# First two units of retention in chunks of 128 tokens, the first weight tiles by halves, the first tile's products begun on half of X, and accumulators evacuated in pairs

## The chip, the cores and the metric

One core of one Trainium2 chip runs the kernel. Its engines are TensorE (PE in the profile; its weight loads are PEld), VectorE (DVE), ScalarE (ACT), GpSimd (POOL) and the queue of DMA issues (SP). The metric is the device time of one execution in microseconds (us); less is better.

## The reference, cut to what matters

```
ret = (q @ k.T / 8) * gamma[h] ** (i - j), zero where j > i     # 4 batches, 8 heads, 576 tokens, head size 64
x   = (ret @ v), heads side by side                             # 2304 x 512
x   = leaky_relu(x @ w_in, 0.01) @ w_out                        # 512 -> 2048 -> 512
out = silu(x @ w2_in) @ w2_out                                  # 512 -> 2048 -> 512
```

The matrices of the two layers arrive as 64-bit floats; everything else is float32.

## The kernel before, in words

**Units.** Retention is done in chunks of 64 tokens (`CH`). A unit is one batch's first 256 tokens (A) or last 320 (B). For each unit and each group `g` of four heads (two pairs `p`) PE makes scores and the chunks' k-v products (`products`; tile `r`), DVE multiplies the scores with a mask of decays (`pt`) and chains the states chunk by chunk (`decay`; `first`, `st`, `sa`), PE makes the outputs (`outer`, `values`; tile `o`), and DVE scales them into `X`. k is scaled beforehand (`scale_k`, on ACT for the very first group, on POOL for the other three). The first two units, A of batch 0 (`u0`) and A of batch 1 (`u1`), fill the first 512 columns of `X`; each has two groups, so there are four group steps before the matrix products of the layers can have all of `X`. The remaining units are worked in between products later on, at places given by the list `ATT_AT`; a unit's loads stand at times in `free`.

**Layers.** A step `t` handles one of 16 slices `f` of the 2048 hidden values for one block of up to 512 tokens. Every float32 operand is split into a high part (`fp32r`, a CAST on ACT) and a remainder (a subtraction on DVE or POOL), and a product is three passes: high by high, high by remainder, remainder by high. `gemm1` makes `h` (four row pieces `c` of `X`, split as `xs`, three passes each: 12 products), `activate` makes `g`, and `gemm2` adds to four accumulators `acc` (12 products) with a lag of `LAG` = 2 steps, so PE's order is h0, h1, h2, acc of 0, h3, acc of 1, h4, and so on. Accumulators live by twos in two PSUM tiles; after the last slice each is copied out, even ones by ACT and odd ones by DVE.

**Weights.** A slice's 64-bit weights (`w`, 128x1024 numbers, 1 MB) come as two DMAs and are decoded to float32 (`wraw`): a scaling on ACT, clamping and shifting on DVE (half of it by an ACT relu), and one combining instruction on DVE (L340). The first half of `wraw` is w_in (split as `wi`), the second w_out (`wo`). For the first 32 steps the order on every engine is the order of the code (`manual_schedule`); behind that a scheduler decides. In the first 16 steps each step also decodes one slice for two steps later. Three buffers hold 64-bit weights, so that a load waits for the decoding three slices back.

`busy` products compute nothing that is used.

Of the kernel before, what the change touches and what calls it, by code (L numbers as in the profile page):

```python
# [23 lines left out]

BUSY = 3
NP = H // 2
# [7 lines left out]
NC = 2 * H + NP  # L34
# [30 lines left out]
def retention_mlp_kernel(ctx: ExitStack, tc: tile.TileContext, qkva, qkvb, w1, w2, consts, out):  # L65
# [26 lines left out]
    gs_sb = cst[:, 2 * H:NC]  # L92
# [68 lines left out]
    def scale_k(u, p):  # L161
        k = raw[u, p][3]
        if (u, p // 2) == (UNITS[0], 0) or u == UNITS[2]:
            for j in range(2):
                nc.scalar.mul(out=k[:, :, j], in_=k[:, :, j], mul=gk_sb[:, 2 * p + j:2 * p + j + 1])
        else:
            engine = nc.gpsimd if u in UNITS[:2] else nc.vector
            g = gk_sb[:, 2 * p:2 * p + 2].unsqueeze(1).unsqueeze(3)
            engine.tensor_tensor(out=k, in0=k, in1=g.to_broadcast(list(k.shape)), op=ALU.mult)

    def products(u, ps):
# [29 lines left out]
        first = u in UNITS[:2]  # L201
        if first:

            st = st_p.tile([128, 2, 64], F32, tag="first", name="first", bufs=4)
            nc.vector.tensor_copy(out=st, in_=t[:, 0, o:o + 256].rearrange("p (i n) -> p i n", i=2)[:, :, :64])
# [15 lines left out]
        if first:
            last[u, ps] = t[:, 1, o:o + 256].rearrange("p (i n) -> p i n", i=2)[:, :, 64:]

    def leave(u, ps):

        x = st_p.tile([128, 2, 64], F32, tag="last", name="last", bufs=4)
        nc.scalar.copy(out=x, in_=last.pop((u, ps)))
        ends.extend((prep[u, p][1], x[:, i], p) for i, p in enumerate(ps))
# [5 lines left out]
    def outer(u, g):  # L234
# [10 lines left out]
        engine = nc.vector if u in UNITS[:2] else nc.gpsimd  # L245
        y = engine.memset(st_p.tile([128, 1], F32, tag="done", name="done"), 0.0)
# [48 lines left out]
    def load_w(layer, f):  # L295

        if layer == 1 and f < 2:
            w = ld_p.tile([128, 1024], F32, tag="ld", name="wraw")
        else:
            w = wraw_p.tile([128, 1024], F32, tag="wraw", name="wraw")  # L300
        wraw[layer, f] = w
        r = dec_p.tile([128, 1024, 2], I32, tag="w64", name="w64")
        src = (w1, w2)[layer][f].bitcast(I32)
        halves = [slice(0, 512), slice(512, 1024)]
        loads = []
        for c in halves:
            loads.append(nc.sync.dma_start(out=r[:, c].rearrange("p n t -> p (n t)"), in_=src[:, 2 * c.start:2 * c.stop]))
        for c in halves if (layer, f) == (0, 0) else [slice(0, 1024)]:
            wdec.append((w[:, c], r[:, c]))
        return loads[0]  # L310
# [32 lines left out]
    def split_wi(layer, i, f):  # L343
# [3 lines left out]
        return split(w[:, 0], w[:, 1], wraw[layer, f][:, :512], nc.gpsimd if (layer, i, f) == (0, 0, 0) else nc.vector)  # L347
# [309 lines left out]
```

## Time and profile before

| | us |
|---|---|
| median of 3 runs (lowest, highest) | 880.05 (879.78, 881.25) |
| the profiled execution | 880.94 |
| its span, first to last instruction | 879.2 |
| PE busy in it | 855.6 |
| mean granted TensorE clock | 0.998 |

The profiled execution is 1.7 us longer than its span, and 0.9 us longer than the median of the runs. Times below count from the start of the span.

### The profile page before, as it was taken

The numbers are of one execution on the slowest core, as the hardware profiler recorded it, in microseconds if no ns is written. First come the engines' busy times: TensorE is split into PE (matmuls) and PEld (weight loads), VectorE is DVE, ScalarE is ACT, GpSimd is POOL, SyncE is SP. The second block draws the span as 40 slices with busy tenths as digits, with TensorE's granted clock in tenths as the row PEclk, the third lists the DMA queues.
The fourth block names the chain that finished last, engine by engine and source line by source line (L and its number), as shares of the span: only waits on it lengthen the run. The fifth ranks groups of instructions, "written<-read, shape, count | busy, mean of one in ns | idle before, by whom it ended". The sixth has DMA issues, their size and how long they took to land.

```text
span 879.2 us, 14579 instructions
## 1 busy us (share of the span) xinstructions
PE 855.6 (97%) x6000; PEld 717.5 (82%) x6000; DVE 535.3 (61%) x928; ACT 442.8 (50%) x766; POOL 10.5 (1%) x27
## 2 busy tenths in 40 slices
PE   4899999999999999999999999999999999999997
PEld 4578778998877877888999888888888888888896
DVE  4688875576455564446999554654465445544575
ACT  2687754454333443445666444544454445444564
POOL 2100000000000000000000000000000000000000
PEclk9999999999999999999999999999999999999999
DMA  7576541221012010101561000010001000100010
GB/s 294 205 258 229 186 160 57 87 83 57 1 59 87 24 52 30 48 1 48 193 238 49 1 0 1 1 48 1 1 1 48 1 0 1 48 1 0 25 25 25
DMA packets 17826, 58.75 MB, mean 67 GB/s; under 512 B 2016, under 2 KB 2144, under 8 KB 17760
## 3 DMA queue, kind: packets, MB, share of 16 engines
q1 hardware_dynamic: 17760, 57.82, 18.8%
q8 instruction: 47, 0.77, 0.4%
q14 instruction: 19, 0.16, 0.1%
HBM read 53.09 MB, written 4.72 MB: 66 GB/s over the span
## 4 chain that ended last, share of the span: by engine, by line
PE 91%; DVE 1%; ACT 1%; issue 0%; DVEq 0%
PE acc L129 44%; PE h L129 43%; PE o L129 2%; PE r L129 2%; DVE wraw L340 0%; ACT X L414 0%; DVE st L231 0%; DVE g L108 0%; DVE y L418 0%; ACT g L107 0%; ACT wo L107 0%; DVE wi L108 0%; ACT hs L384 0%; ACT y L420 0%; DVE xs L108 0%
## 5 line engine op out<-in xcount | busy, mean ns | idle before, releaser
L129 PE MATMUL h<-xs,wi 128*128 128x512 f32 (+3 forms) x1920 | 432.6, 370 | 1.9 <-ACT wi L107 1.8
L129 PEld LDWEIGHTS h<-xs,wi 128*128 128x128 f32 x1920 | 341.9, 188 | 61.5 <-ACT wi L107 2.7
L129 PE MATMUL acc<-g,wo 128*128 128x512 f32 (+2 forms) x960 | 218.4, 372 | 1.4 <-ACT X L414 1.4
L129 PE MATMUL acc<-wo,g 128*128 128x512 f32 x864 | 212.8, 390 | 0.7 <-ACT y L420 0.7
L129 PEld LDWEIGHTS acc<-g,wo 128*128 128x128 f32 x960 | 171.5, 188 | 28.7 <-ACT X L414 2.2
L129 PEld LDWEIGHTS acc<-wo,g 128*128 128x128 f32 x864 | 161.0, 188 | 33.8 <-ACT y L420 1.1
L107 ACT CAST wo<-wraw 128x512 fp32r<-128x512 f32 x160 | 99.4, 621 | 136.4 <-PE acc L129 136.2
L108 DVE TENSOR_TENSOR wo<-wraw,wo 128x512 fp32r<-128x512 f32 x160 | 110.4, 690 | 94.2 <-ACT wo L107 93.5
L108 DVE TENSOR_TENSOR wi<-wraw,wi 128x512 fp32r<-128x512 f32 x159 | 109.2, 687 | 54.0 <-ACT wi L107 51.9
L387 DVE TENSOR_TENSOR hs<-h,hs 128x512 f32<-128x512 f32 (+1 forms) x80 | 51.0, 638 | 107.2 <-ACT hs L386 107.1
L108 DVE TENSOR_TENSOR g<-hs,g 128x512 fp32r<-128x512 f32 (+3 forms) x160 | 101.6, 635 | 17.0 <-ACT g L107 12.9
L386 ACT ACTIVATE hs<-h 128x512 f32<-128x512 f32 (+1 forms) x80 | 44.4, 555 | 122.2 <-PE h L129 122.0
L107 ACT CAST wi<-wraw 128x512 fp32r<-128x512 f32 x160 | 98.1, 613 | 15.2 <-DVE wraw L340 15.2
L107 ACT CAST g<-hs 128x512 fp32r<-128x512 f32 (+3 forms) x160 | 93.5, 584 | 11.2 <-DVE hs L387 10.6
L384 ACT ACTIVATE hs<-h 128x512 f32<-128x512 f32 (+2 forms) x80 | 44.3, 554 | 107.1 <-PE h L129 104.6
L319 ACT ACTIVATE wraw<-w 128x1024 f32<-128x1024 f32 (+1 forms) x33 | 36.7, 1111 | 14.5 <-DVE wo L108 8.3
L324 DVE TENSOR_SCALAR w<-w 128x512 uint16<-128x512 uint32 (+1 forms) x32 | 33.5, 1047 | 12.1 <-ACT wraw L319 12.0
L340 DVE SCALAR_TENSOR_TENSOR wraw<-w,wraw 128x1024 int32<-128x1024 int32 (+1 forms) x33 | 39.3, 1190 | 1.6 <-ACT w L330 1.4
L107 ACT CAST xs<-X 128x512 fp32r<-128x512 f32 (+3 forms) x40 | 22.7, 578 | 6.5 <-DVE X L275 5.1
L108 DVE TENSOR_TENSOR xs<-X,xs 128x512 fp32r<-128x512 f32 (+3 forms) x38 | 23.5, 635 | 3.3 <-ACT xs L107 3.1
L330 ACT ACTIVATE w<-w,seven 128x512 uint16<-128x512 uint32 (+1 forms) x15 | 23.0, 1535 | 0.0
L129 PEld LDWEIGHTS r<-qkv 64*64 64x64 f32 x896 | 15.5, 134 | 8.2 <-issue 4.6
(55 smaller groups left out, 241.4 us busy)
## 6 DMA issues: line engine op xcount, KB each, us to landing
w<-in_w SPq DMA_DIRECT2D x64, 512.0 KB, 4.6
qkv<-in_qkvb SPq DMA_DIRECT2D x16, 672.0 KB, 5.4
qkvk<-in_qkva SPq DMA_DIRECT2D x16, 256.0 KB, 5.2
qkv<-in_qkva SPq DMA_DIRECT2D x8, 512.0 KB, 4.3
out<-y SPq DMA_DIRECT2D x15, 256.0 KB, 2.0
out<-y SPq DMA_DIRECT2D x6, 128.0 KB, 2.4
cst<-in_consts SPq DMA_DIRECT2D x1, 138.0 KB, 2.2
```

Source lines behind the costliest of these rows:

```text
L107: yield nc.scalar.copy(out=hi, in_=src)
L108: yield engine.tensor_tensor(out=lo, in0=src, in1=hi.bitcast(F32), op=ALU.subtract)
L129: return nc.tensor.matmul(out, lhsT, rhs, start=start, stop=stop)
L319: yield nc.scalar.mul(out=w, in_=hi.bitcast(F32), mul=2.0 ** -112)
L324: yield nc.vector.tensor_scalar(out=end[:, c], in0=lo[:, c].bitcast(U32), scalar1=2.0 ** -29, scalar2=7.0, op0=ALU.mult, op1=ALU.min)
L330: yield nc.scalar.activation(out=end[:, c], in_=lo[:, c].bitcast(U32), func=AF.Relu, scale=-2.0 ** -29, bias=seven)
L340: yield nc.vector.scalar_tensor_tensor(out=wi, in0=hi, scalar=-0x7FFFFFF9, in1=wi, op0=ALU.bitwise_and, op1=ALU.bitwise_xor)
L384: yield nc.scalar.activation(out=hs[:, :n], in_=h[:, :n], func=AF.Prelu, alpha=0.01)
L386: yield nc.scalar.activation(out=hs[:, :n], in_=h[:, :n], func=AF.Sigmoid)
L387: yield nc.vector.tensor_tensor(out=hs[:, :n], in0=h[:, :n], in1=hs[:, :n], op=ALU.mult)
```

## The change

For the first two units, chunks are 128 tokens long. Scores become products of 128x128 (`scores2`), masked with a new 128-wide mask (`mask2`, made by POOL and DVE at the start); the only state inside a unit is the first chunk's k-v product, copied by ACT (`states2`, tile `kv`), and the outputs are 64x128 products (`values2`) scaled with `gq2`, which POOL makes. The state at a unit's end is worked out later (`end2`). The `busy` products between them go; four of them, on a zeroed tile, stand at PE's start. Weight slice 0 is decoded by halves as before; slices 1 and 2 are loaded and decoded by halves, the first halves (w_in) ahead. The first six products of h0 stand behind the last output group in PE's order, and X's other half is split meanwhile. The split of `wi` for slice 0 moves behind the scaling of k on POOL, and that of slice 1 goes to POOL too. `evacuate` copies accumulators out in pairs, and blocks of two accumulators use one from each PSUM tile. k of a later unit is scaled right behind the work ahead of it (`at + 0.05`).

```diff
-NC = 2 * H + NP
+NC = 4 * H + 3 * NP
...
+    mask2 = wraw_p.tile([128, H, 128], F32, tag="wraw", name="mask2")
+    nc.vector.memset(mask2, 1.0)
+    nc.gpsimd.affine_select(
+        out=mask2, in_=mask2, pattern=[[0, H], [1, 128]], compare_op=ALU.is_ge, fill=0.0, base=0, channel_multiplier=-1)
+    gq2 = g_p.tile([128, NP, 2, CH], F32, tag="g", name="gq2")
...
+        gk = gk2_sb if u in UNITS[:2] else gk_sb
...
+    def scores2(u, g):
+
+        s = banks(u, "r")
+        ps = 2 * g, 2 * g + 1
+        for i, p in enumerate(ps):
+            q, k, _, _ = raw[u, p]
+            for c in range(2):
+                cs = slice(c * 128, (c + 1) * 128)
+                for j in range(2):
+                    mm(s[:, j, i * 256 + c * 128:i * 256 + (c + 1) * 128], k[HALF[j], cs], q[HALF[j], cs], True, True)
+        pt = ld_p.tile([128, 2, 2, 2, 128], F32, tag="ld", name="pt")
+        for i, p in enumerate(ps):
+            y = nc.vector.tensor_tensor(
+                out=pt[:, i], in0=s[:, :, i * 256:(i + 1) * 256].rearrange("p j (c n) -> p j c n", n=128),
+                in1=mask2[:, 2 * p:2 * p + 2].unsqueeze(2).to_broadcast([128, 2, 2, 128]), op=ALU.mult)
+        prep[u, g, "pt"] = pt
+        return y
+
+    def states2(u, g):
+        kv = ps_p.tile([128, 512], F32, tag="ps", name="kv")
+        for i in range(2):
+            _, _, v, kn = raw[u, 2 * g + i]
+            for c in range(2):
+                for j in range(2):
+                    mm(kv[HALF[j], (2 * i + c) * 64:(2 * i + c + 1) * 64], kn[:, c, j], v[:, c, j], True, True)
+        x = st_p.tile([128, 2, 2, 64], F32, tag="first", name="first", bufs=4)
+        nc.scalar.copy(out=x, in_=kv[:, :256].rearrange("p (i c n) -> p i c n", c=2, n=64))
+        prep[u, g, "kv"] = x
+        for i in range(2):
+            ends.append((u[1], 2 * g + i, x[:, i]))
+
+    def values2(u, g):
+        o = banks(u, "o")
+        pt, x = prep[u, g, "pt"], prep[u, g, "kv"]
+        for c in range(2):
+            for j in range(2):
+                for i in range(2):
+                    mm(o[HALF[i], j, c * 128:(c + 1) * 128], raw[u, 2 * g + i][2][:, c, j], pt[:, i, j, c], c == 0, False)
+        for i in range(2):
+            for j in range(2):
+                mm(o[HALF[i], j, 128:256], x[HALF[j], i, 0], raw[u, 2 * g + i][0][HALF[j], 128:256], False, True)
+        y = X[:, 2 * g:2 * g + 2, POS[u]:POS[u] + CA]
+        nc.vector.tensor_tensor(
+            out=y.rearrange("p j (c n) -> p j c n", n=128), in0=o[:, :, :CA].rearrange("p j (c n) -> p j c n", n=128),
+            in1=gq2[:, 2 * g:2 * g + 2].rearrange("p a c n -> p a (c n)").unsqueeze(2).to_broadcast([128, 2, 2, 128]),
+            op=ALU.mult)
...
+        nc.vector.scalar_tensor_tensor(
+            out=sa, in0=x[:, 0], scalar=gs2_sb[:, p:p + 1], in1=x[:, 1], op0=ALU.mult, op1=ALU.add)
...
+    def load_w(layer, f, parts=(0, 1), x=None):
...
+        for i in parts:
+            y = nc.sync.dma_start(out=w64[layer, f][:, i * 512:(i + 1) * 512].rearrange("p n t -> p (n t)"),
+                                  in_=src[:, i * 1024:(i + 1) * 1024])
+            if x is not None:
+                behind(y, x)
+        if len(parts) == 2:
+            wdec.append((wraw[layer, f], w64[layer, f]))
+
+    def half(f, i, by_act):
+
+        c = slice(i * 512, (i + 1) * 512)
+        return decode(wraw[0, f][:, c], w64[0, f][:, c], by_act)
...
-        return split(w[:, 0], w[:, 1], wraw[layer, f][:, :512], nc.gpsimd if (layer, i, f) == (0, 0, 0) else nc.vector)
+        return split(w[:, 0], w[:, 1], wraw[layer, f][:, :512], nc.gpsimd if (layer, i) == (0, 0) and f < 2 else nc.vector)
...
-            t = [acc_p.tile([128, 2, 512], F32, tag=f"acc{m}", name=f"acc{m}") for m in range((nt + 1) // 2)]
-            acc[layer, i] = [t[m // 2][:, m % 2] for m in range(nt)]
+            t = [acc_p.tile([128, 2, 512], F32, tag=f"acc{m}", name=f"acc{m}") for m in range(2)]
+
+            acc[layer, i] = [t[m // 2][:, m % 2] if nt > 2 else t[m][:, 0] for m in range(nt)]
...
-            if f < NF - 1:
-                yield
-                continue
-            if layer == 0:
-                if m % 2:
-                    nc.vector.tensor_copy(out=X[:, m, p0:p0 + n], in_=a[:, :n])
-                else:
-                    nc.scalar.copy(out=X[:, m, p0:p0 + n], in_=a[:, :n])
-            else:
-                y = y_p.tile([128, 512], F32, tag="y", name="y")
-                if m % 2:
-                    nc.vector.tensor_copy(out=y, in_=a)
-                else:
-                    nc.scalar.copy(out=y, in_=a)
-                for o, ln, r in rows_of(p0 + m * 128, 128):
-                    nc.sync.dma_start(out=out[r:r + ln], in_=y[o:o + ln])
+            if f == NF - 1 and (m % 2 or nt < 3):
+                for e in (m,) if nt < 3 else (m - 1, m):
+                    evacuate(layer, p0, n, e, acc[layer, i][e])
             yield
...
+    def evacuate(layer, p0, n, m, a):
+        if layer == 0:
+            y = X[:, m, p0:p0 + n]
+            a = a[:, :n]
+        else:
+            y = y_p.tile([128, 512], F32, tag="y", name="y")
+        if m % 2:
+            nc.vector.tensor_copy(out=y, in_=a)
+        else:
+            nc.scalar.copy(out=y, in_=a)
+        if layer == 1:
+            for o, ln, r in rows_of(p0 + m * 128, 128):
+                nc.sync.dma_start(out=out[r:r + ln], in_=y[o:o + ln])
...
+    nw = 3
...
-    nc.vector.memset(warm[:, :1], 0.0)
+    nc.vector.memset(warm, 0.0)
     nc.scalar.copy(out=warm[:, :1], in_=warm[:, :1])
...
+    def busy(n, size=256):
+
+        for _ in range(n):
+            mm(t[:, :size], warm[:, :128], warm[:, :size], True, True)
+
     u0, u1 = UNITS[:2]
     nc.sync.dma_start(out=cst, in_=consts)
-    more_weights(1)
+    load_w(0, 0, (0,))
+    load_w(0, 0, (1,))
     for g in range(NG):
         for u in (u0, u1):
             for p in (2 * g, 2 * g + 1):
                 load(u, p)
+    load_w(0, 1, (0,))
+    busy(3, 512)
+    busy(1)
     nc.vector.tensor_tensor(
-        out=mask, in0=mask, in1=gn_sb.unsqueeze(2).to_broadcast([128, H, CH]), op=ALU.mult)
-    decodes()
-    more_weights(2)
+        out=mask2, in0=mask2, in1=gn2_sb.unsqueeze(2).to_broadcast([128, H, 128]), op=ALU.mult)
+    nc.gpsimd.tensor_copy(out=gq2[:, :, 0], in_=gq_sb)
+    nc.gpsimd.tensor_tensor(
+        out=gq2[:, :, 1], in0=gq_sb, in1=gr_sb.unsqueeze(2).to_broadcast([128, NP, CH]), op=ALU.mult)
+    for i in range(2):
+        run(half(0, i, 0))
...
     scales(u0, 0)
-    run(split_wi(0, 0, 0))
     scales(u1, 0)
     scales(u0, 1)
     scales(u1, 1)
-    sums(u0, 0)
-    leave(u0, (0, 1))
-    outer(u0, 0)
-    values(u0, 0)
-    sums(u1, 0)
-    leave(u1, (0, 1))
-    outer(u1, 0)
-    sums(u0, 1)
-    leave(u0, (2, 3))
-    x = values(u1, 0)
-
-    more_weights(4, x)
+    scores2(u0, 0)
+    states2(u0, 0)
+    run(split_wi(0, 0, 0))
+    values2(u0, 0)
+    scores2(u1, 0)
+    states2(u1, 0)
+    scores2(u0, 1)
+    values2(u1, 0)
+    states2(u0, 1)
+    values2(u0, 1)
     for c in range(2):
         split_x(0, 0, c)
-    outer(u0, 1)
-    busy(1)
-    sums(u1, 1)
-    second = decode(*wdec.pop(0), 1024)
+    x = scores2(u1, 1)
+
+    for n, (f, i) in enumerate(((2, 0), (1, 1), (2, 1))):
+        load_w(0, f, (i,), x if n == 0 else None)
+    states2(u1, 1)
+    second = half(1, 0, 512)
     next(second)
     next(second)
-    busy(2)
-    values(u0, 1)
-    outer(u1, 1)
-    next(second)
-    busy(2)
-    values(u1, 1)
-    busy(BUSY)
+    values2(u1, 1)
+    h0 = gemm1(0, 0, 0)
+    next(h0)
+    next(h0)
+    run(second)
+    wi1 = split_wi(0, 0, 1)
     for c in range(2, KC):
         split_x(0, 0, c)
-    leave(u1, (2, 3))
+    run(wi1)
+    nc.gpsimd.tensor_tensor(
+        out=mask, in0=mask, in1=gn_sb.unsqueeze(2).to_broadcast([128, H, CH]), op=ALU.mult)
...
-    free = [0.3, 0.8, 1.3]
+    free = [0.3, 1.3, 2.3]
...
-                queue.append((at + d / 2, (f, x)))
+                queue.append((at + 0.05, (f, x)))
...
-        if t == 0:
-            run(second)
-            more_weights(5)
-            run(split_wi(*steps[1]))
-        for n, _ in enumerate(gemm1(l, i, f)):
+        for n, _ in enumerate(h0 if t == 0 else gemm1(l, i, f)):
             attend(t + (n + 1) / 8)
         a = activate(l, i, f)
         if first:
 
-            d = decode(*wdec.pop(0), 512) if t + 2 < NF else iter(())
+
+            d = iter(())
+            if t == 0:
+                d = half(2, 0, 0)
+            elif t + 2 < NF:
+                d = decode(*wdec.pop(0), 512)
             next(d, None)
             next(a)
             next(d, None)
...
             run(wo)
             next(d, None)
             if t + 2 < NF:
-                more_weights(min(NF, t + 6))
+                more_weights(min(NF, t + (4, 4, 5, 6)[min(t, 3)]))
             wi = split_wi(*steps[t + 2])
-            next(a)
-            next(wi)
+            if t == 0:
+                next(wi)
+                next(a)
+                run(wi)
+            else:
+                next(a)
+                next(wi)
             wo = split_wo(l, i, f)
 
 
...
                 attend(t + (n + 5) / 8)
         if first:
             run(wi)
+            if t == 0:
+                run(wo)
+            if t < 2:
+                run(half(1 + t, 1, 512))
             if ends_block:
                 next(wo)
         else:
...
                 split_x(l2, i2, f - (NF - KC))
         if t == 2:
 
-            for before, x, p in ends:
-                decay(before[4], before[3], x, p)
+            for x in ends:
+                end2(*x)
```

On PE, at the program's start, up to the second group's scores (`r` scores, `kv` the k-v products, `o` outputs, `pt` masked scores, `first`, `st`, `sa` states). Before:

```order
L129 MATMUL r<-qkvk 64x64 x32
L129 MATMUL o<-pt,qkvk 64x64 x16
L129 MATMUL o<-qkvk,first 64x64 x4
L129 MATMUL o<-qkvk,st 64x64 x4
L129 MATMUL o<-qkvk,sa 64x64 x4
L129 MATMUL r<-qkvk 64x64 x32
```

On PE at the same place, of the change:

```order
L135 MATMUL busy<-warm 128x512 x3
L135 MATMUL busy<-warm 128x256
L135 MATMUL r<-qkvk 128x128 x8
L135 MATMUL kv<-qkvk 64x64 x8
L135 MATMUL o<-pt,qkvk 64x128 x8
L135 MATMUL o<-qkvk,first 64x128 x4
L135 MATMUL r<-qkvk 128x128 x8
L135 MATMUL kv<-qkvk 64x64 x8
```

A group has 28 products of larger shapes in place of 60, behind four `busy` ones.

On POOL, from the masks to the end of its early work. Before:

```order
L100 AFFINE_SELECT mask<-mask 64x512 x2
L108 TENSOR_TENSOR wi<-wraw,wi 128x512
L169 TENSOR_TENSOR qkvk<-qkvk,cst 128x256 x6
L108 TENSOR_TENSOR xs<-X,xs 128x512 x2
L246 MEMSET done<- 128x1 x12
```

On POOL, of the change:

```order
L106 AFFINE_SELECT mask<-mask 64x512 x2
L521 COPY gq_111<-cst 128x4x64
L522 TENSOR_TENSOR gq_111<-cst 128x4x64
L102 AFFINE_SELECT mask_108<-mask_108 128x1024
L176 TENSOR_TENSOR qkvk<-qkvk,cst 128x256 x6
L114 TENSOR_TENSOR wi<-wraw,wi 128x512
L114 TENSOR_TENSOR xs<-X,xs 128x512 x2
L114 TENSOR_TENSOR wi<-wraw,wi 128x512
L564 TENSOR_TENSOR mask<-mask,cst 128x512
```

The select of `mask2` stands behind the two instructions that make `gq2`, and the first split of `wi` behind all scaling of k.

On ACT, of the change, from the high part of wi for slice 1 on (`w_311` is slice 2, `w_151` slice 1, `w_376` slice 3; `hs` is h0's activation in the first row of that name and h1's in the second):

```order
L113 CAST wi<-wraw 128x512
L372 ACTIVATE wraw<-w_311 128x512
L437 ACTIVATE hs<-h 128x512
L113 CAST g<-hs 128x512
L113 CAST wi<-wraw 128x512
L113 CAST wo<-wraw 128x512
L372 ACTIVATE wraw<-w_151 128x512
L383 ACTIVATE w_151<-w_151,seven 128x512
L372 ACTIVATE wraw<-w_376 128x1024
L437 ACTIVATE hs<-h 128x512
L383 ACTIVATE w_376<-w_376,seven 128x512
```

Before, no half of an earlier slice stood between the `wo` cast and the next slice's scaling; now slice 1's second half does, and one step later slice 2's.

## Rows read from the trace of the kernel before

**Rows 1.** The chain that ended last, shares of the span by engine.

```profile
PE 91%; DVE 1%; ACT 1%; issue 0%; DVEq 0%
```

**Rows 2.** What PE waited for: us in total, times, longest us.

```profile
PE r L129 <- DMA qkvk<-in_qkva: 8.2, 2, 7.6
...
PE h L129 <- ACT wi L107: 1.8, 2, 1.5
...
PE r L129 <- ACT qkv L165: 1.5, 1, 1.5
PE acc L129 <- ACT X L414: 1.4, 2, 0.7
...
PE acc L129 <- ACT y L420: 0.7, 1, 0.7
```

**Rows 3.** PE in order of time, to 70 us: start us, us, what.

```profile
14.26 1.88 PE L129 MATMUL r<-qkvk 64*64 64x64 f32 x64
...
24.20 1.16 PE L129 MATMUL r<-qkvk 64*64 64x64 f32 x64 [0.64 <-DVE done L246]
...
32.30 3.11 PE L129 MATMUL h<-xs,wi 128*128 128x512 f32 x12
...
51.89 1.52 PE L129 MATMUL h<-xs,wi 128*128 128x512 f32 x6
53.34 0.81 PE L129 MATMUL r<-qkv 64*64 64x64 f32 x40
54.08 1.66 PE L129 MATMUL h<-xs,wi 128*128 128x512 f32 x6
...
66.75 2.89 PE L129 MATMUL h<-xs,wi 128*128 128x512 f32 x12
```

**Rows 4.** Stretches: PE busy (instructions), granted clock, DMA share, GB/s.

```profile
24.15:27.40 3.25, 3.19 (x125) 1.00 0.50 146
14.30:16.30 2.00, 1.84 (x72) 1.00 1.07 411
21.00:22.00 1.00, 1.00 (x49) 0.50 0.06 16
24.30:25.30 1.00, 1.00 (x65) 1.00 0.13 29
```

**Rows 5.** POOL in order of time, to 45 us.

```profile
1.57 1.36 POOL L100 TENSOR_SCALAR_AFFINE_SELECT mask<-mask 64x512 f32<-64x512 f32 x2 [1.06 <-DVE warm L443]
10.84 1.27 POOL L108 TENSOR_TENSOR wi<-wraw,wi 128x512 fp32r<-128x512 f32 x1 [7.91 <-ACT wi L107]
...
17.27 0.61 POOL L169 TENSOR_TENSOR qkvk<-qkvk,cst 128x256 f32<-128x256 f32 x1 [0.61 <-DMA qkvk<-in_qkva]
```

**Rows 6.** DVE in order of time, to 15 us.

```profile
3.17 0.69 DVE L456 TENSOR_TENSOR mask<-mask,cst 128x512 f32<-128x512 f32 x1 [1.67 <-DMA cst<-in_consts]
5.99 0.73 DVE L324 TENSOR_SCALAR w<-w 128x512 uint16<-128x512 uint32 x1 [2.13 <-ACT wraw L319]
...
7.61 0.74 DVE L324 TENSOR_SCALAR w<-w 128x512 uint16<-128x512 uint32 x1
...
14.55 0.69 DVE L275 TENSOR_TENSOR X<-o,cst 128x512 f32<-128x512 f32 x1 [1.48 <-PE o L129]
```

**Rows 7.** ACT in order of time, one step of the early layer.

```profile
40.91 1.13 ACT L319 ACTIVATE wraw<-w 128x1024 f32<-128x1024 f32 x1
41.92 0.60 ACT L384 ACTIVATE hs<-h 128x512 f32<-128x512 f32 x1
42.40 1.47 ACT L330 ACTIVATE w<-w,seven 128x512 uint16<-128x512 uint32 x1
...
45.18 0.62 ACT L107 CAST wi<-wraw 128x512 fp32r<-128x512 f32 x1 [0.88 <-DVE wraw L340]
```

**Rows 8.** DMAs issued at L307 from 24 to 27 us.

```profile
L307 SPq DMA_DIRECT2D w<-in_w x4: 328/404/622, 24.2 to 25.5; - x4
...
DMA to landing us min/median/max: 4.6/7.2/8.3
```

More of the change, by code (lines that the diff above doesn't have):

```diff
@@ L23 @@
 LAG = 2
-BUSY = 3
 NP = H // 2
@@ L162, in scale_k @@
         k = raw[u, p][3]
+        gk = gk2_sb if u in UNITS[:2] else gk_sb
         if (u, p // 2) == (UNITS[0], 0) or u == UNITS[2]:
             for j in range(2):
[L165 removed]
+                nc.scalar.mul(out=k[:, :, j], in_=k[:, :, j], mul=gk[:, 2 * p + j:2 * p + j + 1])
         else:
             engine = nc.gpsimd if u in UNITS[:2] else nc.vector
[L168 removed]
+            g = gk[:, 2 * p:2 * p + 2].unsqueeze(1).unsqueeze(3)
             engine.tensor_tensor(out=k, in0=k, in1=g.to_broadcast(list(k.shape)), op=ALU.mult)
@@ L200, in products @@
             prep[u, p] = pt
[L201 to L205, printed above, removed]
         for i, p in enumerate(ps):
@@ L210, in products @@
                 sa = st_p.tile([128, 64], F32, tag="sa", name="sa", bufs=2 * NP)
-                before = [None, st[:, i] if first else x[:, 0], x[:, 1], sa if first else x[:, 2], sa]
+                before = [None, x[:, 0], x[:, 1], x[:, 2], sa]
                 state[u[1], p] = sa
-                if not first:
-                    nc.vector.tensor_copy(out=x[:, 0], in_=k[0])
+                nc.vector.tensor_copy(out=x[:, 0], in_=k[0])
             else:
@@ L217, in products @@
                 before = [state[u[1], p]] + [x[:, c] for c in range(4)]
-            for c in range(1 if u[0] == "A" else 0, 3 if first else 4):
+            for c in range(1 if u[0] == "A" else 0, 4):
                 decay(before[c + 1], before[c], k[c], p)
             prep[u, p] = prep[u, p], before
[L221 to L228, printed above, removed]
+    def scores2(u, g):
[14 more added lines that the diff above has]
+        return y
@@ L230, in decay, with end2 @@
+    def end2(b, p, x):
+        sa = st_p.tile([128, 64], F32, tag="sa", name="sa", bufs=2 * NP)
+        state[b, p] = sa
+        nc.vector.scalar_tensor_tensor(
+            out=sa, in0=x[:, 0], scalar=gs2_sb[:, p:p + 1], in1=x[:, 1], op0=ALU.mult, op1=ALU.add)
     def decay(out, state, kv, p):
@@ L243, in outer @@
                        prep[u, p][0][HALF[c % 2], j, c // 2], c < 2, False)
-        engine = nc.vector if u in UNITS[:2] else nc.gpsimd
-        y = engine.memset(st_p.tile([128, 1], F32, tag="done", name="done"), 0.0)
+        y = nc.gpsimd.memset(st_p.tile([128, 1], F32, tag="done", name="done"), 0.0)
         behind(y, x)
@@ L293, in retention_mlp_kernel @@
     acc = {}
-    def load_w(layer, f):
-        if layer == 1 and f < 2:
-            w = ld_p.tile([128, 1024], F32, tag="ld", name="wraw")
-        else:
-            w = wraw_p.tile([128, 1024], F32, tag="wraw", name="wraw")
-        wraw[layer, f] = w
-        r = dec_p.tile([128, 1024, 2], I32, tag="w64", name="w64")
-        src = (w1, w2)[layer][f].bitcast(I32)
[L304 to L310, printed above, removed]
+    w64 = {}
+    def load_w(layer, f, parts=(0, 1), x=None):
+        if (layer, f) not in w64:
+            p, tag = (ld_p, "ld") if layer == 1 and f < 2 else (wraw_p, "wraw")
+            wraw[layer, f] = p.tile([128, 1024], F32, tag=tag, name="wraw")
+            w64[layer, f] = dec_p.tile([128, 1024, 2], I32, tag="w64", name="w64")
+        src = (w1, w2)[layer][f].bitcast(I32)
+        for i in parts:
[8 more added lines that the diff above has]
+        return decode(wraw[0, f][:, c], w64[0, f][:, c], by_act)
     def decode(w, r, by_act=0):
@@ L448, in retention_mlp_kernel @@
     ordered.enter_context(tc.manual_schedule())
+    t = ps_p.tile([128, 512], F32, tag="ps", name="busy")
+    def busy(n, size=256):
+        for _ in range(n):
+            mm(t[:, :size], warm[:, :128], warm[:, :size], True, True)
     u0, u1 = UNITS[:2]
     nc.sync.dma_start(out=cst, in_=consts)
-    more_weights(1)
+    load_w(0, 0, (0,))
+    load_w(0, 0, (1,))
     for g in range(NG):
@@ L463, in scales @@
             scale_k(u, p)
-    def sums(u, g):
-        products(u, (2 * g, 2 * g + 1))
-    t = ps_p.tile([128, 512], F32, tag="ps", name="busy")
-    def busy(n):
-        for _ in range(n):
-            mm(t[:, :256], mask[:, 0:2], mask[:, 0:4], True, True)
     scales(u0, 0)
-    run(split_wi(0, 0, 0))
     scales(u1, 0)
```

18 lines of the change are left out of this document (9 added, 9 removed).

## The prediction

> **What bounds the kernel now.** I read the chain that ended last first: PE is 91% of it [rows 1], so the time is PE's work plus what PE waits. The waits of PE say where there is anything to win [rows 2]: 8.2 us until the first q and k land, a few waits up to 64 us (of these 1.5 for the scaling of k on ACT), and only three of 0.7 later, behind copies out of accumulators (2 x 0.7 X, 1 x 0.7 y). In PE's order of time [rows 3] the first real product of the layers, h0, starts at 32.30 and h6 at 66.75. From h6 on PE is full but for those three waits, so whatever makes h6 earlier comes off the end one for one. That stretch has two parts: what happens before h0 (32.30), and h0 to h6 (34.45).
>
> **What PE's attention products cost.** At 24.20 us 32 products of 64x64 over 64 columns take 1.16 us; I take 0.2 of it as the run-out of the last (an estimate), so one costs 0.030, four lying side by side in the array. At 14.26 the same 32 take 1.88 us, 0.0525 each [rows 3]. The granted clock reads 1.00 in both stretches, but 0.50 at 21 to 22 us [rows 4], and the first stretch passes products at 39 per us of busy time against 65, so I take it as the lower level, 1.2 GHz. Counting such quarter pieces, a group before has 60 (32 for scores and k-v, 28 for outputs). Now scores are 8 products of 4 pieces, k-v 8 of 2, outputs 8 of 4 and 4 of 2: 88 pieces, 2.64 us at the full clock, 4.6 at the low one, against 1.8 and 3.15. So on PE alone the change adds 3.4 us to four groups. What it takes away is the chain of states on DVE (four decays, a copy and a memset per group) and the low clock: four `busy` products (1792 columns; by 0.0525 for a 64x64 piece, four in a column, 5.9 us) run from about 3.6 (an estimate: DVE first clears 1536 more columns, and ACT copies one) without pause into the scores. I take the full clock from 8 us on. If it came only behind the first group, at 12, h0 would be 1.4 later; at 6.6 nothing would change, since DVE is then the later one.
>
> **Up to h0.** POOL's first selects end at 2.93 [rows 5]; then stand the two for `gq2` (0.45, between nothing and 0.61, and 0.61, the price of a 128x256 product) and the select for `mask2`, twice the size of a pair's half, 1.36: 5.6. DVE multiplies `mask2` with the constants, 1.3 (twice 0.69, less overlap), to 6.9, then decodes slice 0, whose two halves take 1.62 each from start to start [rows 6], to 10.25: 1.0 later than before. Scores of the first group are done by then. A masking of a pair is now 512 wide out of PSUM, 0.69 as the scaling into X [rows 6], 0.62 from start to start. The chain: masks to 11.5; outputs (0.030 x 40 = 1.2) to 12.8; the second group's scores and k-v (1.45) to 14.25, its masks to 15.3, outputs to 16.5; k-v and outputs of the third to 18.2; scores of the fourth to 19.15; its masks, behind the third's scaling into X, to 20.7; its outputs to 21.9. The last k is scaled on POOL at 17.9 [rows 5], early enough. **h0 starts at 21.9**, 10.4 earlier than 32.30.
>
> **h0 to h6.** Twelve products of a tile take 2.72 at the full clock (2.89 less the run-out [rows 3]). h0's first six run at once (POOL's remainders: 1.27 each behind 17.9, so 19.1, 20.4, 21.6, in time). For the other half X is ready at 22.9, its high part at 23.5, its remainder behind slice 1's shift and combine on DVE at 24.6: 1.1 us of wait, h0 ends at 25.8. h1 follows (POOL's remainder of wi at 26.0) to 28.5, h2, but for 0.3, to 31.5, acc of step 0 to 34.2. Then the loads bind. Three halves and slice 3 are issued from the end of the fourth group's masks, 20.7, for which SP now waits; all later loads stand behind that wait. Before, four halves issued from 24.2 landed between 4.6 and 8.3 us after issue [rows 8], about 1.5 apart; in 24.15 to 27.40 the queue moved 146 GB/s, 0.47 MB [rows 4]. So slice 3, the fourth and fifth half, is there at 31.8. A step's scaling, prelu, relu, combine and wi cast cost 4.3 from start to start [rows 7]: wi of slice 3 is out at 36.8 and h3 starts there, 2.6 of wait, 0.3 for its remainder. Slice 2's second half (0.58 and 1.2 on ACT, in front of slice 4) makes slice 1's wo late by 1.9 for the next acc, and two waits of 0.5 remain. With two scorings of 0.75, h6 is at 57.9: 36.0 after h0, against 34.45. The 1.5 for the scaling of k is gone, since that stands one step earlier on ACT. So of the 10.4 about 1.6 is given back: **h6 is 8.8 earlier**.
>
> **The rest.** Copies in pairs leave PE nothing to wait for in the tile it is writing: 1.4 in the first block's end, and 0.7 at the last, where the two accumulators now lie in different tiles [rows 2]. Behind a pair of y copies the next pair waits for the y buffers; the next product into that tile is four us later, so I price that at nothing; without this cover it is under 1. The mask product on POOL, the later `end2` (8 small instructions as before), and slice halves decoded in two rather than one (0.1 each) are hidden behind POOL's idle time and in the step times above. Sum: 8.8 + 1.4 + 0.7 = 10.9. The profiled execution's 880.94 becomes 870.0; it lies 0.9 above the median of the runs, so against 880.05 I say **869.2**.
>
> **Rivals.**
> *The new shapes cost more than pieces side by side.* For: none of these shapes stands in the trace; before, every early product is 64x64. Against: four pieces do lie side by side there, and a row of scores between two halves of a tile, at 51.89, 53.34 and 54.08 [rows 3], loses only 0.09 on the six products of 1.36 in front. If scores alone go one after the other, h0 is 3.1 later: 872.3. If all do at the full clock, a group is 5.8, 12.6 more in four, less what fills PE's present waits for masks and loads, 7.1 later: 876.3. Bounds are thus 0 and 7.1. The Trainium skill speaks against the change here: TensorEngine Tiling, Key Properties, says that switching the tiling mode drains the engine, and the new groups switch 13 times. By that rule it would be about 871; the 0.09 in the row says less.
> *The clock stays low until the layers' products.* For: from 14.3 to 16.3 us PE was busy 1.84 of 2.00 before [rows 4], and still slow. Against: `busy` has no gap. 4.6 a group, 7.8 more in four less the same waits, puts h0 near 29: 876.
> *The loads come sooner or later.* If halves land in their order at the 411 GB/s of a full stretch [rows 4], slice 3 is there by 29.2 and only the ACT chain binds: 1.8 earlier, 867.4. Two us later gives 871.2.
> *Slower.* Low clock and one product after another together are one thing to PE, a product at 0.21 for each 64 columns as it would cost alone at 1.2 GHz: 10.1 a group, 30 more in four, h0 at about 47 and the time near 894. It decides from about 6 us a group. The 24.20 row against the 14.26 row speaks against it.
> *Nothing.* ACT's step is near PE's own pace: 4.3 to the wi cast [rows 7] and 0.5 each for it and wo, against 5.4 for 24 products. If the halves cost it a further 2 us in each of the first five steps, all is given back: 880.
>
> **Chances.** Forecast, 866.5 to 871.5: 0.60 (0.08 of it with a run-out at each of the 13 changes of shape, 2.6 less what waits for masks cover, near 871). Better, by loads in order: 0.08. Dearer shapes, late loads or low clock, 871.5 to 877: 0.22. No change 0.03, slower 0.07. The range 865.5 to 874.5 leaves out the far half of the third case, the last two and a little below, about 2 in 10. 0.2% (1.8 us) is about what a measurement here can tell from no change; faster than that 0.90, within it 0.03, slower 0.07.
>
> **What would show it.** h0 near 22 and h6 near 58, with PE's long wait in between in front of h3, put down to wi on ACT; scores of a group in about 1 us behind 9 us at granted clock 1.00; no waits for X or y copies. A first layer product after 25, a low clock in the groups, or waits for wo longer than 2 us at each step would make me wrong.

## The result and the profile after

The changed kernel takes 869.07 us (median, 868.84 to 869.32) beside 880.65 for the kernel before in the same measurement: a ratio of 0.9865, with a 95% interval of 0.9845 to 0.9884. The forecast was 869.2. The profiled execution took 869.32, its span is 867.6 (879.2 before), and PE is busy 854.9 of it (855.6): all but 0.7 of the 11.6 is waiting that is gone.

The chain that ended last, and PE's waits over the whole span, where [rows 1, 2] stood before:

```profile
PE 94%; DVE 1%; ACT 0%; issue 0%
```

```profile
PE busy L135 <- ACT warm L496: 3.4, 1, 3.4
PE h L135 <- ACT wi L113: 2.0, 2, 1.3
PE acc L135 <- DVE wo L114: 1.7, 1, 1.7
PE r L135 <- DMA qkvk<-in_qkva: 0.6, 1, 0.6
PE h L135 <- DVE xs L114: 0.6, 1, 0.6
...
```

No wait for X, y or a scaled k is left. PE's order of time, where [rows 3] stood before:

```profile
3.39 5.19 PE L135 MATMUL busy<-warm 128*128 128x512 f32 x8 [3.39 <-ACT warm L496]
8.56 0.72 PE L135 MATMUL r<-qkvk 64*128 64x128 f32 x8
9.91 0.71 PE L135 MATMUL r<-qkvk 64*128 64x128 f32 x8 [0.63 <-DMA qkvk<-in_qkva]
...
13.41 1.16 PE L135 MATMUL r<-qkvk 64*128 64x128 f32 x16
14.50 0.69 PE L135 MATMUL kv<-qkvk 128*64 128x64 f32 x16
15.12 1.16 PE L135 MATMUL r<-qkvk 64*128 64x128 f32 x16
16.21 1.09 PE L135 MATMUL o<-pt,qkvk 128*64 128x128 f32 x16
17.23 0.45 PE L135 MATMUL o<-qkvk,first 64*64 64x128 f32 x8
17.61 0.69 PE L135 MATMUL kv<-qkvk 128*64 128x64 f32 x16
18.12 1.05 PE L135 MATMUL o<-pt,qkvk 128*64 128x128 f32 x16
...
23.43 2.04 PE L135 MATMUL h<-xs,wi 128*128 128x512 f32 x7
26.03 4.31 PE L135 MATMUL h<-xs,wi 128*128 128x512 f32 x17 [0.56 <-DVE xs L114]
31.07 3.33 PE L135 MATMUL h<-xs,wi 128*128 128x512 f32 x12 [0.74 <-ACT wi L113]
...
38.37 3.30 PE L135 MATMUL h<-xs,wi 128*128 128x512 f32 x12 [1.25 <-ACT wi L113]
...
43.83 2.60 PE L135 MATMUL acc<-g,wo 128*128 128x512 f32 x10 [1.70 <-DVE wo L114]
...
59.08 2.88 PE L135 MATMUL h<-xs,wi 128*128 128x512 f32 x12
```

h0 starts at 23.43 instead of 32.30, 8.9 earlier; h6 at 59.08 instead of 66.75, 7.7 earlier. So 1.2 is given back in between, net of the waits that stood there before; the long waits are now three, for wi at h2 and h3 and for wo behind h3. The span, however, is 11.6 shorter, so 3.9 more is won behind h6, where the forecast had 2.1. Three places hold it, found by comparing the start of each product from h6 on (as many in both): 1.9 at the end of the first block, 0.9 around the second block's end, 1.1 in the last copies.

PE's order of time at the first two places in the kernel before:

```profile
137.59 0.98 PE L129 MATMUL acc<-g,wo 128*128 128x512 f32 x3
139.25 1.65 PE L129 MATMUL acc<-g,wo 128*128 128x512 f32 x6 [0.68 <-ACT X L414]
141.58 0.96 PE L129 MATMUL acc<-g,wo 128*128 128x512 f32 x3 [0.68 <-ACT X L414]
142.38 1.47 PE L129 MATMUL h<-xs,wi 128*128 128x320 f32 x9
...
215.77 0.56 PE L129 MATMUL r<-qkv 64*64 64x64 f32 x18
216.26 0.71 PE L129 MATMUL acc<-g,wo 128*128 128x320 f32 x3
216.89 0.33 PE L129 MATMUL r<-qkv 64*64 64x64 f32 x2
...
217.78 0.56 PE L129 MATMUL r<-qkv 64*64 64x64 f32 x20
```

and in the changed one:

```profile
129.92 3.06 PE L135 MATMUL acc<-g,wo 128*128 128x512 f32 x12
132.81 1.48 PE L135 MATMUL h<-xs,wi 128*128 128x320 f32 x9
...
206.64 0.81 PE L135 MATMUL r<-qkv 64*64 64x64 f32 x40
```

From its first product to the next h, the same twelve products take 4.79 before (137.59 to 142.38) and 2.89 after (129.92 to 132.81). The two waits are listed with 0.68 each, but cost 0.95 each. The first three products start 1.66 ahead of the fourth, where three in a row take 0.7 (0.23 from start to start). The listed idle time begins only where the last product's record ends, 0.40 behind its start and so 0.17 behind the start that the next one could have had; and in the single records the first product behind the wait stands 0.34, not 0.23, ahead of its successor. Together 0.68, 0.17 and 0.11 are 0.96. The rows at 215.77 show the second place: before, the scheduler cut one group of scores into 18, 2 and 20 around products of acc; after, the 40 stand together.

### The profile page after: what moved, and what is told of

It reads as the page before. It is cut to its first block, busy times and chain, and to the rows that moved or that the text cites. A ratio compares the mean times of both kernels' runs of the same rounds, so it can differ in the third digit from the quotient of the medians.

```text
span 867.6 us, 14043 instructions
## 1 busy us (share of the span) xinstructions
PE 854.9 (99%) x5736; PEld 714.9 (82%) x5736; DVE 536.4 (62%) x907; ACT 445.8 (51%) x769; POOL 16.0 (2%) x32
## 4 chain that ended last, share of the span: by engine, by line
PE 94%; DVE 1%; ACT 0%; issue 0%
PE acc L135 45%; PE h L135 45%; PE o L135 2%; PE r L135 2%; DVE st L280 0%; DVE g L114 0%; DVE y L473 0%; ACT g L113 0%; DVE wi L114 0%; DVE wo L114 0%; ACT hs L437 0%; DVE xs L114 0%; DVE pt L204 0%; ACT xs L113 0%; DVE wraw L390 0%
## 5 line engine op out<-in xcount | busy, mean ns | idle before, releaser
L135 PE MATMUL acc<-g,wo 128*128 128x512 f32 (+2 forms) x960 | 216.1, 371 | 1.7 <-DVE wo L114 1.7
L135 PE MATMUL acc<-wo,g 128*128 128x512 f32 x864 | 209.9, 389 | 0.0
L383 ACT ACTIVATE w<-w,seven 128x512 uint16<-128x512 uint32 x16 | 23.3, 1456 | 0.1
```

What stands on the lines that cost most here:

```text
L135: return nc.tensor.matmul(out, lhsT, rhs, start=start, stop=stop)
L383: yield nc.scalar.activation(out=end[:, c], in_=lo[:, c].bitcast(U32), func=AF.Relu, scale=-2.0 ** -29, bias=seven)
```

## The experiments

Times of h0, h6 and what lies between are from each run's profile; the medians and ratios are of whole executions, the ratio against the kernel before in the same measurement (medians there 879.89 for b_pairs to a_pool, 880.45 for the last four).

| run | h0 | h6 | between | median us | ratio (95%) |
|---|---|---|---|---|---|
| before | 32.30 | 66.75 | 34.45 | 880.65 | 1 |
| changed | 23.43 | 59.08 | 35.65 | 869.07 | 0.9865 (0.9845, 0.9884) |
| b_pairs | 30.67 | 65.11 | 34.44 | 876.50 | 0.9962 (0.9951, 0.9974) |
| a_nobusy | 23.52 | 59.02 | 35.50 | 870.12 | 0.9892 (0.9875, 0.9908) |
| a_loads | 23.39 | 58.88 | 35.49 | 869.31 | 0.9879 (0.9864, 0.9894) |
| a_turn | 29.70 | 65.24 | 35.54 | 875.07 | 0.9944 (0.9929, 0.9958) |
| b_busy | 28.97 | 63.46 | 34.49 | 878.56 | 0.9986 (0.9975, 0.9997) |
| a_act | 22.98 | 58.05 | 35.07 | 869.99 | 0.9882 (0.9861, 0.9903) |
| a_late | 22.88 | 58.55 | 35.67 | 868.58 | 0.9872 (0.9852, 0.9892) |
| a_pool | 23.28 | 58.27 | 34.99 | 869.96 | 0.9882 (0.9862, 0.9903) |
| a_again | 23.66 | 59.34 | 35.68 | 869.17 | 0.9873 (0.9857, 0.9889) |
| a_wo | 22.77 | 58.46 | 35.69 | 869.56 | 0.9876 (0.9860, 0.9893) |
| a_five | 23.25 | 56.79 | 33.54 | 866.61 | 0.9840 (0.9826, 0.9855) |
| a_five_nobusy | 22.47 | 56.33 | 33.86 | 867.02 | 0.9845 (0.9830, 0.9860) |

**The ends of blocks.** b_pairs is the kernel before with `gemm2` and `evacuate` of the changed one.

> The kernel before with the copies in pairs and the last block's two accumulators in separate tiles, nothing else. If the late gain of the change is these waits and the pauses around them: 1.9 us at the first block's end and 1.1 at the last, 3.0 in all, a ratio near 0.9966. If the 0.9 us that the changed kernel also gains near the second block's end (where one group of scores before is cut in three by products of acc) belongs to the pairs too: 3.9 us, 0.9956. By the forecast's own sum only 2.1 us, 0.9976. If these waits were not on the path: 1.000.

```profile
135.98 3.06 PE L129 MATMUL acc<-g,wo 128*128 128x512 f32 x12
138.87 1.48 PE L129 MATMUL h<-xs,wi 128*128 128x320 f32 x9
...
212.70 0.81 PE L129 MATMUL r<-qkv 64*64 64x64 f32 x40
```

PE's order of time in b_pairs: the block's end takes 2.89 and the 40 scores stand together, as in the changed kernel. Behind h6 its last product is 4.0 earlier relative to before, of which 0.7 is lost again behind that product in this execution. The ratio of 0.9962 is 3.3 us of 880 (2.3 to 4.3). So the late gain belongs to this part of the change alone, the uncut group of scores too, and that piece of it is an outcome of the scheduler's order. Its earlier h0 (30.67) goes with PE's waits put down to "issue", 1.4 in all here and 3.7 in the profile of before.

**The clock at the start.** a_nobusy leaves out the four products at PE's start; b_busy adds them alone to the kernel before.

```diff
-    busy(3, 512)
-    busy(1)
```

> The changed kernel without the four busy products at the start. Clock theory: before, PE's products ran at half pace from the first one at 7.6 us until 15.95; from 8.6 here that would be until about 17, so the first two groups go at half pace (about 3 us more each, part of it under waits for q, k and masks) and h0 starts 3 to 4 us later, near 27, time near 872.5; if the clock falls again as it did before at 19.4, h0 near 29 and 876. Rival, the first groups are bound by loads and DVE anyway: h0 within 0.5 of 23.4 and the time within 0.5 of the changed kernel.

> The kernel before with the four busy products at the start alone (its chunks of 64 stay). Clock theory: before, the products of the first groups ran at half pace until 15.95 and again from 19.37 to 22.78 us; at the full one a group costs 1.8 rather than 3.15, so as far as PE is what is waited for h0 starts 2 to 4 us earlier and the time is 876 to 878 beside 880. If the early clock is worth nothing (as leaving the busy products out of the changed kernel cost 0.1 at h0): h0 within 1 of before and the time within 0.5. If the clock were most of the change's front gain: h0 near 24 and 872.

PE's order of time in a_nobusy:

```profile
8.09 2.57 PE L135 MATMUL r<-qkvk 64*128 64x128 f32 x16 [8.09 <-DMA qkvk<-in_qkva]
...
13.50 1.16 PE L135 MATMUL r<-qkvk 64*128 64x128 f32 x16
```

The first scores go at half pace, and yet the first group's outputs end where they do with busy: the second group starts at 13.50 against 13.41, because the first group waits for q, k and masks anyway. (The granted clock reads 1.00 from 8.10 to 10.50 all the same; the pace of the rows is what tells the two apart.) From 13.50 on the chunks of 128 go at the same pace as with busy. In this execution busy is worth 0.1 at h0, within the spread of 0.9 over runs that stands further down; the medians, 870.12 and 869.07 with intervals that overlap, leave up to some 1 us open. The clock theory's 3 to 4 us falls. In the kernel before busy helps, by 0.14% (0.03 to 0.25, 1.2 us), but its stretches of b_busy (us, PE busy, granted clock, DMA share, GB/s) show that it doesn't keep the clock there, among PE's waits for masks and states:

```profile
8.00:11.00 3.00, 1.49 (x52) 1.00 1.04 396
13.00:15.00 2.00, 2.00 (x80) 0.50 1.05 404
16.00:19.00 3.00, 2.38 (x120) 1.00 1.02 406
```

So the front's gain is neither the early clock alone nor mainly that. What is left is the shorter chain: h0 at 23.4 with or without busy, against 29.0 with the early clock and chunks of 64. No run takes that chain apart into its pieces.

**The price of a change of shape.** a_turn lets score and k-v products of the last group alternate.

```diff
                     mm(s[:, j, i * 256 + c * 128:i * 256 + (c + 1) * 128], k[HALF[j], cs], q[HALF[j], cs], True, True)
+                    mm(kv[HALF[j], (2 * i + c) * 64:(2 * i + c + 1) * 64], kn[:, c, j], v[:, c, j], True, True)
```

> The changed kernel with the score and the k-v products of the fourth group one by one in turn rather than eight and eight: the same products, 15 changes of shape rather than one. Pieces theory (the forecast's): the 16 products take 1.7 us as before (1.09 and 0.62 from start to start), masks stand 0.6 later, h0 at most 0.6 later, time within 0.6. Run-out theory: a change of shape costs about 0.12 us (a group takes 3.1 us against 2.64 worked out, over four changes), so 14 more cost 1.7, the 16 products take 3.4, h0 starts 1.7 to 2.3 later and the time is near 871. If shapes only exclude each other's side by side (each product alone in the array): 16 products at 0.107 to 0.21, about 2.6 us, h0 about 1.5 later.

Its order of time on PE (each product has two records), and two stretches with the columns of the last view:

```profile
19.22 0.48 PE L135 MATMUL r<-qkvk 64*128 64x128 f32 x2
19.64 0.33 PE L135 MATMUL kv<-qkvk 128*64 128x64 f32 x2
19.89 0.48 PE L135 MATMUL r<-qkvk 64*128 64x128 f32 x2
...
26.56 2.57 PE L135 MATMUL o<-pt,qkvk 128*64 128x128 f32 x16 [0.38 <-DVE pt L270]
```

```profile
19.20:21.90 2.70, 2.70 (x20) 1.00 0.03 8
22.70:26.10 3.40, 3.40 (x13) 0.50 0.00 0
```

A score and a k-v product take 0.67 in turn (19.22 to 19.89) and 0.21 in rows of eight ((1.09 + 0.62) / 8): 0.23 for each change of shape, with what is lost of lying side by side in it. From 22.7 on the granted clock reads 0.50, though PE was never idle ahead of it, and the outputs take 2.57 instead of 1.09. h0 is 6.3 later, about three times what the run-out theory expected. By the Trainium skill, TensorEngine Tiling, Key Properties, a switch of the tiling mode drains the engine; this row agrees, and gives it a price. Eight products in a row pay less. In the changed kernel the second group's 3.11 (1.09 + 0.62 + 1.02 + 0.38 from start to start) against 2.64 worked out from pieces is four changes at 0.12; the third group, with three, takes 2.96. The changed kernel's own rows show the price without that working: k-v products take 0.62 when scores of another tile shape follow (14.50 to 15.12; 128*64, then 64*128) and 0.51 when outputs of the same tile shape follow (17.61 to 18.12), and all eleven profiles of kernels with these chunks have 0.61 to 0.62 against 0.51 to 0.52. So one change costs 0.1 there, and it is the change of the tile's shape that costs, not that of the kind of product.

**What binds between h0 and h6.** a_loads moves the weights' wait one group forward (`x` from `scores2(u0, 1)`); a_pool moves POOL's product of `mask` from behind `wi1` to the start; a_act takes ACT's share out of two second halves; a_wo puts wo's remainder of slice 1 first on DVE. What these four and a_late gain is read from one profiled execution each: by whole executions (medians 868.58 to 869.99) none of them is told from the changed kernel (869.07, and 869.17 in a_again).

```diff
-    x = scores2(u1, 1)
+    x = scores2(u0, 1)
...
+    nc.gpsimd.tensor_tensor(
+        out=mask, in0=mask, in1=gn_sb.unsqueeze(2).to_broadcast([128, H, CH]), op=ALU.mult)
     def scales(u, g):
...
-                run(half(1 + t, 1, 512))
+                run(half(1 + t, 1, 0))
...
-            if t == 0:
-                run(wo)
             if t < 2:
+                run(wo)
```

> The changed kernel with the three weight loads waiting for the third group's masks rather than the fourth's, issued at about 17.6 rather than 22.0 us. Load theory (the forecast's): the first half of slice 2 is there at about 23 rather than 27.5, PE's 0.74 before h2 goes, and of the 1.25 before h3 and the 1.70 for wo behind it a part: 1 to 3.5 us faster, 866 to 868. ACT theory: ACT's row from 27.5 to 36.7 us has no pause but one of 1.1, so what is won before h2 is waited for later: within 0.5. Collision theory: the loads take the queue from the last k, which POOL scales at 18.71, and h0 comes up to 1.3 later.

> The changed kernel with POOL's product of the second mask at about 5 us, where POOL is idle, rather than at 27.7. Contention theory: DVE's pass over the low words at 28.22 took 1.12 beside that product and 0.74 elsewhere, so wi of slice 2 comes 0.4 earlier, the 0.74 before h2 falls to about 0.35 and the time by 0.4. If POOL costs DVE nothing, or if what is won is given back before h3: within 0.1 at h6.

> The changed kernel with the second halves of slices 1 and 2 decoded without ACT's share (DVE does the 512 columns, 0.74 and 0.46 there, in place of 1.46 on ACT and 0.42 on DVE). ACT theory: ACT's row from 30 to 45 us has hardly a pause, so PE's 1.27 before h3 goes and the 1.70 for wo falls to about 0.5: 1.5 to 3 us faster, 866 to 867.6. DVE theory: DVE, full from 26 to 33 us, is as late as ACT, and the wait moves to it: within 0.5. Load theory (the forecast's 2.6 before h3): no change, since slice 3 lands no sooner.

> The changed kernel with DVE's remainder of slice 1's wo ahead of its work on slice 2's second half and slice 4, at about 39 rather than 43.1 us. Order theory: PE's 1.70 before acc at 43.83 is only DVE's order, it goes; h4 then waits for wi of slice 4 (cast from 44.94 to 45.56 on ACT), so h4 starts at about 45.6 rather than 46.26, 0.7 earlier, and the time falls by 0.7. ACT theory: wo's cast is what is late, the wait stays: no change. If nothing else waits: 1.7 less.

In the changed kernel ACT waits 1.50 for slice 2's load. In a_loads it no longer does (its scaling starts at 25.89 instead of 27.52), yet wi comes only 0.2 earlier. DVE in the changed kernel at the start, then DVE and POOL of a_loads, in order of time, show why:

```profile
8.58 0.74 DVE L377 TENSOR_SCALAR w<-w 128x512 uint16<-128x512 uint32 x1 [0.58 <-ACT wraw L372]
9.12 0.45 DVE L387 TENSOR_SCALAR wraw<-wraw 128x512 int32<-128x512 int32 x1
```

```profile
26.60 1.70 DVE L377 TENSOR_SCALAR w<-w 128x512 uint16<-128x512 uint32 x1
28.09 1.30 DVE L387 TENSOR_SCALAR wraw<-wraw 128x512 int32<-128x512 int32 x1
```

```profile
26.06 1.62 POOL L114 TENSOR_TENSOR wi<-wraw,wi 128x512 fp32r<-128x512 f32 x1 [3.06 <-ACT wi L113]
27.64 1.46 POOL L564 TENSOR_TENSOR mask<-mask,cst 128x512 f32<-128x512 f32 x1
```

DVE's two passes take 0.74 and 0.45 at 8.58 us, where POOL is idle; here 1.70 and 1.30, each ending 0.3 to 0.6 behind POOL's instruction. The Trainium skill, SBUF — State Buffer, Who interferes with whom, says that a tensor_scalar of DVE can take the pair of ports that DVE shares with GpSimd, and that whichever engine issues first then has the pair for its whole instruction while the other is blocked. The rows agree, and POOL's own instructions grew too (1.27 to 1.62 for a remainder of wi, 1.04 to 1.46 for the mask's product). With the mask's product at 5 us (a_pool) the second pass takes 0.45, the wait before h2 is gone and the stretch is 0.66 shorter. A part of this is an earlier load: ACT scales slice 2 from 26.50 in that run, from 27.52 in the changed kernel. a_nobusy keeps the product in its old place and has that load almost as early (26.74); its second pass takes 1.31, and its stretch is 35.50. The second pass in a_nobusy, then in a_pool:

```profile
28.24 1.31 DVE L387 TENSOR_SCALAR wraw<-wraw 128x512 int32<-128x512 int32 x1
```

```profile
28.00 0.45 DVE L387 TENSOR_SCALAR wraw<-wraw 128x512 int32<-128x512 int32 x1
```

So the early load alone gives 0.15, and the mask's product is worth some 0.5. a_act brings 0.58, where its ACT theory gave 1.5 to 3: the wait before h3 falls from 1.25 to 0.41, that for wo grows from 1.70 to 2.11. In a_wo the wait for wo is gone, a new one of 1.27 for wi stands before h4, and by h6 nothing of it is left. So these waits hang together on DVE and ACT, and what is won at one largely comes back at the next. The loads are not out of it. Before h2 slice 2's load does stand in the chain, but taking it out wins only 0.2, since DVE's work beside POOL is as late; before h3 ACT waits for none. Where ACT is early, slice 4's load comes next. ACT at slice 4 in a_act, where DVE and so wo's remainder are late by it, and in a_five (below):

```profile
39.62 1.12 ACT L372 ACTIVATE wraw<-w 128x1024 f32<-128x1024 f32 x1 [1.67 <-DMA w<-in_w]
```

```profile
38.39 1.14 ACT L372 ACTIVATE wraw<-w 128x1024 f32<-128x1024 f32 x1 [1.16 <-DMA w<-in_w]
```

**The start.** a_late loads slice 0's second half behind q, k and v.

```diff
-    load_w(0, 0, (1,))
...
+    load_w(0, 0, (1,))
     load_w(0, 1, (0,))
...
-    for i in range(2):
-        run(half(0, i, 0))
+    run(half(0, 0, 0))
...
+    run(half(0, 1, 0))
     states2(u1, 1)
```

> The changed kernel with the second half of slice 0 (512 KB) loaded behind all q, k and v rather than ahead of them, and decoded behind the last group's masks. Theory: PE is full from 13 us to h0 and the first group waits for the second pair's q and k, so 512 KB less in front of them at some 390 GB/s make all of it 1.3 us earlier: h0 at 22.1, and 867.8. If the start is bound by DVE's constants and decoding rather: 0.5 or less. If what is won is given back before h2 or h3 on ACT and DVE: h0 earlier by 1.3, h6 by less than 0.5, time as the changed kernel's.

h0 came at 22.88, but the profiles of the kernels that leave the start alone (changed, a_again, a_loads, a_act, a_wo) have it anywhere from 22.77 to 23.66: nothing can be told. The spread begins with the first loads: in these five ACT starts on slice 0's second half, which stands ahead of q and k, at 6.86 (a_wo) to 8.11 (a_again). In a_late no wait of PE for q and k is left and scores start at 8.91, when busy ends; but a_act and a_wo, with the start as it was, show no such wait either (9.01 and 8.80).

**All together.** a_again is the changed kernel, a_five has the five edits, a_five_nobusy drops busy as well.

> The changed kernel itself once more, as the measure for the next three and for how much its start differs from run to run: h0 within 0.5 of 23.43, h6 within 0.8 of 59.08, ratio 0.9865 to 0.988.

> The changed kernel with five edits together: slice 0's second half loaded and decoded late, weight loads waiting for the third group, POOL's mask product at 5 us, second halves without ACT's share, wo's remainder in front. Alone they gave 0.5, 0.2, 0.8 and 1.0 at h6 (the fifth not yet timed). If they add up, as waits of different places in one chain: h0 at 22.8, no wait before h2 and for wo, under 0.5 before h3, h6 at 55.5 to 56.3, 865.5 to 866.5. If what each gains is what the next then waits for: h6 at 57.5 to 58, 867.5.

> The same five edits without the busy products at the start. With slice 0's second half out of the way the first q and k are there at about 7 us, and busy holds PE until 8.9. If that order is what binds: the first scores start at 7, at half pace, and h0 0.3 to 0.8 earlier than with busy. If the half pace (until 12.2 without busy in the other order) now binds: h0 0.5 to 1 later. If neither, the same within 0.2.

PE's longest waits in a_five behind h0:

```profile
PE h L135 <- ACT wi L113: 1.4, 2, 1.1
```

The stretch from h0 to h6 is 33.54, 2.1 less than in the changed kernel, where the edits alone gave 0.66, 0.58, 0.16 and twice nothing. No wait for wo is left; that its removal, worth nothing alone, pays once ACT is early too is a reading that no run with these two alone tests. The 1.1 that is left stands before h4 and goes back to the load of slice 4, for which ACT waits 1.16 (row above). 866.61 beside 869.17 is 0.3%, with intervals that just don't touch (0.9855 and 0.9857). It beats both kernels. DVE's first pass on slice 2 still takes 1.72 there, beside POOL's remainder of wi. h0 gained nothing, since busy ended at 9.3 in that run. Without busy the first scores start at 6.72 at half pace and h0 at 22.47; the medians (866.61, 867.02) don't tell the two apart.

## Why the prediction was right

**h0 at 21.9.** Measured 23.43. The chain was right (scores, masks, outputs, group after group on PE, no wait for k), the term for a group too small: 2.64 assumed, 3.11 and 2.96 measured. At 0.11 to 0.12 for a change of shape the forecast's 13 changes are 1.5, part of it under the waits for masks. The other part of the 1.5 is the first group: the second one's scores start at 13.41 instead of 12.8, since the second q and k came 1 us later than before (9.91 against 8.87 in PE's rows). That belongs to the spread of the first loads over runs. In a_wo, whose first loads came earliest, the second group's scores start at 12.74, near the forecast, and h0 at 22.77: the 0.9 left there goes with the shapes. Why the loads spread is open.

**The full clock from 8 us, by busy.** The products kept the full pace, but the step that made busy a condition failed: "4.6 a group ... puts h0 near 29" without it. a_nobusy has h0 at 23.52.

**Loads bind before h3.** This step failed: the forecast had 0.3 at h2, 2.6 plus 0.3 at h3 and 1.9 for wo; measured are 0.74, 1.25 and 1.70. Only wo's is near, and it was DVE's order that made it (a_wo), not ACT alone. Slice 3 landed about when the forecast had it (its second half at 32.7 by the trace, 31.8 forecast), but ACT came to it only at 33.35, without a wait for it, and a_loads, with earlier loads, has it at 33.16 and changes the whole stretch by 0.2. The sum was close (1.2 given back, 1.6 forecast), but the cause is mainly DVE and ACT; of the loads only slice 2's stands in the chain, before h2, for 0.2. The rival by which the loads' order would give 1.8 falls with it.

**The mask product and slice halves hidden.** Not so for the product: on POOL it cost DVE, and by way of it PE, some 0.5. The slice halves were not tried alone.

**Copies in pairs 2.1.** Right in kind, too small: 3.0 for the three waits, since a listed wait of 0.68 costs 0.95 to 1.1, and 0.9 more from the scheduler's order, which was not in the sum.

**Dearer shapes.** The forecast left this to a rival with bounds of 0 and 7.1; the true price, 1.5 before what waits cover, is nearer the low bound; the kernel keeps eight products of a shape together. The row that the forecast argued from held this price already. It took the 0.09 in front of the scores (51.89 to 53.34) and left out what stands behind them: the whole of it, 51.89 to 55.58 in before, is 3.69, which less 2.72 for the twelve products and 0.60 for twenty scores leaves 0.37 for two changes of shape. a_turn shows the other end.

So 869.2 against 869.07 is partly luck: a front 1.1 dearer and an end 1.8 cheaper than worked out. A third part of the luck is the median: the execution profiled before stood 0.9 above its own, the one after 0.25 above, so that 11.6 between the profiles and the forecast's 10.9 come out at the same figure. How much of the front's 7.7 is special to the profiled execution of before, whose "issue" waits were 3.7 against 1.4 in b_pairs, can only be bounded: by whole executions a_again's 0.9873 is 11.2 us, and less the 3.3 of b_pairs some 8 is left for the front, give or take 2 (an estimate from the two intervals). That h0 begins on half of X was not undone by itself; before, too, h0 started at 32.30 while DVE still made the remainders of X's other half (32.57 to 33.86), so that little can hang on it. Nor were the old kernel's own filler products taken out alone, which hold PE for 4.0 ahead of its h0 (0.70, 1.06, 1.06 and 1.21), in part in place of waits: what the gain owes to them and what to the longer chunks is not shown.

## What to carry to other kernels

Price a wait of PE from the start of the product ahead to the start of the product behind it, less their usual distance; the idle time listed misses the last product's run-out. Keep products of one tile shape in rows: here a change cost 0.1 behind eight together, 0.23 when they alternated, and then the clock fell too. Before calling a wait a load's, move the load: here that won 0.2, because DVE's work beside POOL's was as late.

## What was not expected of the hardware

DVE's passes more than doubled beside POOL's products (0.74 to 1.70, 0.45 to 1.30). The chunks of 128 reached the full pace by 13.5 us without any filler, while the granted clock fell to 0.50 behind alternating shapes with PE busy 2.70 of 2.70 us. The length of the same four busy products at the start differed from 4.8 (b_busy) to 6.0 us (a_five) between runs.
